# Inputs laid out by the host, small first weight pieces, and clears on GpSimd, in a kernel of two attention blocks

## The chip, the cores and the metric

The kernel runs on one core of one Trainium2 chip. The metric is the device time of one execution in microseconds (us), measured for whole executions; lower is better. A profile is one execution recorded by the hardware profiler; its span (first to last instruction) is about 1.7 us shorter than the measured time of the same execution. Engines: PE (TensorE, matmuls), PEld (its weight loads), DVE (VectorE), ACT (ScalarE), POOL (GpSimd), SP (SyncE, which here only issues transfers). Runs of one kernel scatter by about 1%; a run over 1.5% above the fastest of its kernel is called slow and is left out of every ratio. Work that the host does beforehand is not in this time.

## The reference, cut to what matters

Two attention blocks on 2048 tokens of width 640, with 32 heads of 20, bf16 inputs; their outputs are put side by side.

```
A: q, k, v = x@wq, x@wk, x@wv ; 4 segments of 512 tokens
   within a segment: causal softmax attention
   plus a memory read  phi(q)@M / (phi(q)@z)  gated per head by sigmoid(beta); M, z grow with each segment
   output @ wo
B: q, k, v = x@wqkv ; softmax over a causal window of 256 tokens ; output @ wo
```

The softmax exponentials are the largest single group of the profile (297.9 us): 2 x 32 heads of scores must pass through ACT.

## The kernel before

Work is cut into eight chunks of 512 tokens (A0, B0, A1, B1, ...). All instructions are emitted in an order that a small list scheduler inside the program chooses while the program is built. It keeps an estimated clock for each engine (`f.pe`, `f.act`, `f.dve`, ...), estimated times at which loaded data is there (`mark`), and a chain of pseudo-random choices that starts anew from a given seed every ten score batches:

```python
ORDER = (29069, 0, 182751, 884974, 439894, 0, 228057, 646802, 512461, 772592, 0, 0, 0, 0, 894820)
STRETCH = 10
...
    def stretch(self, i):
        x = i // STRETCH
        self.x = ORDER[x] if x < len(ORDER) else 0

    def pick(self, *of):
        if not self.x:
            return of[0]
        self.x = (self.x * 1103515245 + 12345) % 2147483648
        return of[(self.x >> 12) % len(of)]
```

The engines do not know this clock. Each runs its instructions in the emitted order and waits on semaphores, so an estimate that is wrong does not break the result; it makes an engine wait in front of an instruction while others behind it would have been ready.

The start, which the change rewrites (cut):

```python
        f.dve = f.pool = 6000.0
        f.pe = f.act = 8000.0                    # ns: the scheduler's clock at the first projection
        ...
        nc.vector.memset(zt.bitcast(F32), 0.0)   # 256 columns of qB, for the warm-up
        get_x(0)                                 # dma_start_transpose of x
        # first pieces (172 columns) of wk, wq on ACT's queue, the rest on SP's
        self.load_beta(A_beta)                   # also computes exp(-beta) on ACT
        for x in range(17):                      # warm-up matmuls on zeros
            nc.tensor.matmul(ps[:, :], lhsT=zt[:, 0:P], rhs=zt, start=True, stop=True)
        ...
        nc.vector.memset(self.qB[:, 1:G, :].bitcast(F32), 0.0)
        for t in self.kB:
            nc.vector.memset(t[:].bitcast(F32), 0.0)
        ...
        self.mark(22000.0, 1, "x")               # estimated arrival of B's first x
```

The softmax here doesn't subtract the row's maximum and nothing guards it: scores larger than these inputs give would overflow.

## Time and profile before

| kernel before | |
|---|---|
| median of the first 3 runs | 371.14 us (369.25 to 373.62) |
| span of the profile | 368.6 us |
| ACT busy | 329.8 us, 89% |
| first exponential | 11.53 us |
| ACT's exponentials waiting for PE | 19.8 us (18.1 + 1.5 + 0.2) |

The page of the profile gives busy time, share of the span and number of instructions of each engine:

```profile
PE 335.7 (91%) x6679; PEld 179.0 (49%) x6714; DVE 287.0 (78%) x547; ACT 329.8 (89%) x412; POOL 183.1 (50%) x250
```

Its groups of instructions read: line, engine, operation, output and input with shapes, count, busy us, mean ns, then the idle time just before them and what ended it.

```profile
L654 ACT ACTIVATE pt<-sc 128x1024 bf16<-128x1024 f32 (+1 forms) x328 | 297.9, 1038 | 20.1 <-PE sc L644 18.1
```

ACT's exponentials alone are 297.9 us, and ACT waited only 20.1 us in front of them. PE's 91% says less: it includes warm-up and filler matmuls. The list of waits (who waited for what: total us, times, longest) names what the exponentials waited for:

```profile
ACT pt L654 <- PE sc L644: 18.1, 19, 3.7
...
ACT pt L654 <- PE sc L634: 1.5, 4, 0.5
```

A further 0.2 us makes the 19.8 us of the table. The timeline of the start has start us, duration us, engine, line, operation, tiles, count, and in brackets the idle time before and what ended it:

```profile
7.75 1.26 PE L341 MATMUL m_226<-xT,wk_A 128*32 128x512 bf16 x20
...
9.17 0.64 DVE L349 TENSOR_SCALAR kA<-m_226,rowmask 128x512 bf16<-128x512 f32 x1
...
11.10 0.40 PE L644 MATMUL sc<-qA,kA 32*128 32x512 bf16 x4
...
11.53 7.64 ACT L654 ACTIVATE pt<-sc 128x1024 bf16<-128x1024 f32 x8 [0.81 <-PE sc L644]
...
11.89 0.17 DVE L296 TENSOR_SCALAR t_311<-e_85 128x32 f32<-128x32 f32 x1
```

The first projection starts at 7.75 us, the first exponential at 11.53, and from there ACT is nearly always busy. The waits that stand out in the middle belong to PE, in front of pkT, a transposed copy of phi(k) that is loaded back from a scratch in HBM:

```profile
PE m_1684 L513 <- DMA pkT<-scr_pk_206: 3.0, 1, 3.0
PE m_2862 L513 <- DMA pkT<-scr_pk_207: 2.9, 1, 2.9
```

### The profile page before, as it was taken

Reading aid. Unit: us, or ns where it says so; the run is one execution under the profiler, and the core shown is the slowest. Engines: PE = TensorE matmul, PEld = TensorE weight load, DVE = VectorE, ACT = ScalarE, POOL = GpSimd, SP = SyncE. Lnnn points to the kernel's source line nnn. Section 1 sums busy time; section 2 is a strip of 40 time slices with the busy share of each in tenths; the row PEclk is TensorE's granted clock in tenths of the full one; section 3 lists DMA queues with packets and bytes.
Section 4 is the critical chain, followed back from the end, with each engine's and each line's share of the span. In section 5 each row is a group of like instructions: output and inputs, shape, how many; then the busy total and the mean of one; then the engine's idle time right before and its main releaser. Section 6 shows DMA issues by size and latency. Waiting matters only on the chain.

```text
span 368.6 us, 15618 instructions
## 1 busy us (share of the span) xinstructions
PE 335.7 (91%) x6679; PEld 179.0 (49%) x6714; DVE 287.0 (78%) x547; ACT 329.8 (89%) x412; POOL 183.1 (50%) x250
## 2 busy tenths in 40 slices
PE   8999999969799689889999979998999999998997
PEld 3444354544444434455455544554444555655564
DVE  7667896859798568998799778898797878786760
ACT  1889998959899689999999979999999999997954
POOL 4334442423375335575655555557575655656420
PEclk9999999989999899999999999999999999999999
DMA  9975637789494556249848855366644277529653
GB/s 216 295 260 180 175 111 202 168 196 183 129 221 128 127 145 145 80 138 170 235 122 207 195 135 154 111 139 166 173 117 135 55 191 193 128 75 143 164 125 114
DMA packets 104253, 58.49 MB, mean 159 GB/s; under 512 B 68408, under 2 KB 103608, under 8 KB 104120
## 3 DMA queue, kind: packets, MB, share of 16 engines
q1 hardware_dynamic: 102584, 56.97, 61.8%
q8 instruction: 52, 0.85, 1.0%
q10 hardware_dynamic: 1600, 0.53, 0.6%
q14 instruction: 17, 0.14, 0.1%
HBM read 20.16 MB, written 24.58 MB: 121 GB/s over the span
## 4 chain that ended last, share of the span: by engine, by line
PE 43%; ACT 25%; DMA 12%; DVE 11%; issue 6%; SPq 2%; ACTq 0%; DVEq 0%
ACT pt L654 22%; PE sc L644 6%; DVE tt L739 2%; DMA pkT<-scr_pk_206 2%; DVE st L425 2%; DVE st L201 2%; ACT e L417 2%; PE sc L634 1%; DMA pkT<-scr_pk_207 1%; DMA vbot_177<-vB_166 1%; SPq L377 1%; DMA scr_pk_207<-st 1%; DVE o L758 1%; DMA kB_144<-scr_kB_217 1%; DMA scr_kA_200<-st 1%
## 5 line engine op out<-in xcount | busy, mean ns | idle before, releaser
L654 ACT ACTIVATE pt<-sc 128x1024 bf16<-128x1024 f32 (+1 forms) x328 | 297.9, 1038 | 20.1 <-PE sc L644 18.1
L702 POOL TENSOR_SCALAR_AFFINE_SELECT pt<-pt 128x512 bf16<-128x512 bf16 (+1 forms) x144 | 122.9, 853 | 141.4 <-ACT pt L654 140.6
L698 POOL TENSOR_SCALAR_AFFINE_SELECT pt<-pt 128x512 bf16<-128x512 bf16 x56 | 39.5, 706 | 29.7 <-ACT pt L654 29.7
L758 DVE TENSOR_TENSOR o<-tt,rr 128x320 bf16<-128x320 f32 x64 | 43.2, 674 | 0.8 <-DVE rr L764 0.3
L562 PEld LDWEIGHTS <-xT 128*128 128x128 bf16 x400 | 32.5, 97 | 18.9 <-issue 10.2
L644 PE MATMUL sc<-qA,kA 32*128 32x128 bf16 (+3 forms) x512 | 35.8, 302 | 2.0 <-ACT pt L654 1.2
L820 PEld LDWEIGHTS <-oT 128*128 128x128 bf16 x280 | 24.0, 97 | 15.2 <-issue 5.6
L644 PEld LDWEIGHTS <-kA 32*128 32x128 bf16 x512 | 10.8, 92 | 28.2 <-issue 26.0
L683 DVE TENSOR_TENSOR pt<-pt,hmask 128x2048 bf16<-128x2048 bf16 (+1 forms) x20 | 21.1, 1054 | 0.4 <-ACT pt L654 0.4
L777 POOL TENSOR_TENSOR o<-o,u 128x320 bf16<-128x320 bf16 x24 | 20.1, 836 | 0.0
L644 PE MATMUL sc<-qB,kB_143 32*128 32x64 bf16 (+3 forms) x416 | 18.4, 232 | 0.7 <-ACT pt L654 0.7
L764 DVE RECIPROCAL rr<-tt 128x16 f32<-128x16 f32 x88 | 18.4, 231 | 0.6
L425 DVE SCALAR_TENSOR_TENSOR st<-st,e 128x512 bf16<-128x512 bf16 x25 | 18.3, 738 | 0.0
L716 PEld LDWEIGHTS <-vA 128*32 128x32 bf16 x512 | 11.1, 96 | 13.2 <-issue 1.5
L644 PE MATMUL sc<-qB,kB_144 32*128 32x64 bf16 (+3 forms) x480 | 15.4, 213 | 1.3 <-ACT pt L654 1.1
L417 ACT ACTIVATE e<-st 128x512 bf16<-128x512 bf16 x25 | 15.6, 685 | 0.0
L758 DVE TENSOR_TENSOR u<-tt,rr 128x320 bf16<-128x320 f32 x24 | 15.1, 629 | 0.0
L644 PEld LDWEIGHTS <-kB_143 32*128 32x128 bf16 x416 | 7.9, 92 | 12.9 <-issue 11.6
L399 PEld LDWEIGHTS <-wBq 128*128 128x128 bf16 x100 | 8.6, 97 | 11.0 <-issue 3.5
L399 PEld LDWEIGHTS <-wBk 128*128 128x128 bf16 x100 | 8.5, 97 | 10.1 <-issue 2.6
L716 PEld LDWEIGHTS <-vB_171 128*32 128x32 bf16 x480 | 10.0, 96 | 6.5 <-issue 3.4
L716 PEld LDWEIGHTS <-vB_166 128*32 128x32 bf16 x416 | 9.7, 99 | 7.0 <-issue 1.6
(745 smaller groups left out, 676.8 us busy)
## 6 DMA issues: line engine op xcount, KB each, us to landing
out_dram<-ot SPq DMA_DIRECT2D x31, 160.0 KB
wv_A<-in_A_wv_dram SPq DMA_DIRECT2D x2, 400.0 KB
wBk<-in_B_wqkv_dram SPq DMA_DIRECT2D x1, 800.0 KB
wBq<-in_B_wqkv_dram SPq DMA_DIRECT2D x1, 800.0 KB
wBv<-in_B_wqkv_dram SPq DMA_DIRECT2D x1, 800.0 KB
scr_wo_A<-in_A_wo_dram SPq DMA_DIRECT2D x4, 200.0 KB
wo_A<-scr_wo_A SPq DMA_DIRECT2D x1, 800.0 KB
scr_wo_B<-in_B_wo_dram SPq DMA_DIRECT2D x4, 200.0 KB
```

The costliest lines, as they stand in the source:

```text
L417: nc.scalar.activation(out=e[:], in_=x, func=ACT.Exp)
L425: nc.vector.scalar_tensor_tensor(out=out, in0=x, scalar=0.0, in1=e[:], op0=ALU.max, op1=ALU.add)
L562: nc.tensor.matmul(ps[:, c0:c0 + w], lhsT=xT[:, kt, tt * P:(tt + 1) * P], rhs=w_ap[:, kt, a:a + w], start=(kt == 0), stop=(kt == self.KT - 1))
L644: nc.tensor.matmul(ps[j // 2][:, j % 2, c0:c0 + 64 * nb], lhsT=k[rows, g, P * kc:P * kc + P], rhs=q[rows, g, 64 * b0:64 * (b0 + nb)], star ...
L654: nc.scalar.activation(out=pt[:, 2 * i:2 * i + 2, 0:hi], in_=ps[i][:, :, 0:hi], func=ACT.Exp, scale=self.scale)
L683: nc.vector.tensor_tensor(out=pv, in0=pv, in1=m, op=ALU.min)
L698: nc.gpsimd.affine_select(out=blk, in_=blk, pattern=[[0, r], [-1, w]], compare_op=ALU.is_ge, fill=self.zero, base=-1, channel_multiplier=1)
L702: nc.gpsimd.affine_select(out=blk, in_=blk, pattern=[[0, r], [1, w]], compare_op=ALU.is_ge, fill=self.zero, base=128 - w, channel_multipli ...
L716: nc.tensor.matmul(O[HD * j:HD * j + HD, c:c + 64 * nb], lhsT=self.vcols(v, h // 16 if vk[0] == "v" else 0, vt, h, HD), rhs=rhs[j], start= ...
L758: nc.vector.tensor_tensor(out=out, in0=a, in1=b, op=ALU.mult)
L777: nc.gpsimd.tensor_tensor(out=dst, in0=dst, in1=u[:], op=ALU.add)
L820: nc.tensor.matmul(ps[0:w, 0:320], lhsT=oT[:, m, x:x + w], rhs=wo[:, m, 320 * hf:320 * hf + 320], start=(m == 0), stop=(m == self.KT - 1))
```

## The change

The intent is to start earlier and to relieve SP and the DMA engines. The host transposes x per chunk, packs each weight matrix so that a partition's row is contiguous, pads it, and permutes the rows of wo. So eight transposing loads of x become plain ones, and the eight copies of wo through a scratch in HBM go. The first two head groups of wk and wq come as small separate pieces (`hk`, `hq`), nine warm-up matmuls stand in place of 17, and the clears of B's buffers move from DVE to GpSimd. The scheduler's clock and its estimates of loads are set to the new start; the seeds stay as they are. The diff, cut to its core:

```diff
+NWARM = 9
+WK, WQ, WV = (7300.0, 10900.0), (8600.0, 12000.0), (9800.0, 13200.0)
@@ load_wo2 (weights of the last output projection)
-        for j in range(4):
-            self.nc.sync.dma_start(out=self.wk_A[HD * j:HD * j + HD, :, 0:self.D], in_=self.scr_wo[...])
-        self.f.on_dma(4, 1430.0)
+        self.nc.sync.dma_start(out=self.wk_A[:, :, 0:self.D], in_=self.w["wo2"])
+        self.f.on_dma(1, 2400.0)
@@ load_x
-        self.nc.sync.dma_start_transpose(out=t[:], in_=x2d[c * L:(c + 1) * L, :])
+        for a, b in zip(cuts, cuts[1:]):
+            self.nc.sync.dma_start(out=t[:, a:b, :], in_=x4[c, :, a:b, :])
@@ beta: its exponential moves from load_beta to consts_beta, which is emitted later
@@ the scheduler's clock and estimates
-        f.dve = f.pool = 6000.0
-        f.pe = f.act = 8000.0
+        f.dve = f.pool = 5000.0
+        f.pe = f.act = 5500.0
-                self.mark(f.on_dma(1, 100.0, f.pe, 2900.0, 2100.0) + 50.0, n, "x")
+                self.mark(f.on_dma(1, 1900.0, f.pe, 500.0, 1100.0) + 50.0, n, "x")
-        self.mark(22000.0, 1, "x")
-        f.sp = f.ring = 19000.0
+        self.mark(14000.0, 1, "x")
+        f.sp = f.ring = 15000.0
-                while late and f.pe > 12000.0:
+                while late and f.pe > 8000.0:
@@ clears
-        nc.vector.memset(self.qB[:, 1:G, :].bitcast(F32), 0.0)
-        for t in self.kB:
-            nc.vector.memset(t[:].bitcast(F32), 0.0)
+        for t in (self.kB[0][:], self.qB[:, 1:G, :]):
+            nc.gpsimd.memset(t.bitcast(F32), 0.0)
-        nc.gpsimd.memset(self.MZb[:], 0.0)                    # on GpSimd before too, but earlier
-                nc.vector.memset(t[:].bitcast(F32), 0.0)      # vtop, vbot
+                nc.gpsimd.memset(t[:].bitcast(F32), 0.0)
+        nc.gpsimd.memset(self.kB[1][:].bitcast(F32), 0.0)
+        nc.gpsimd.memset(self.MZb[:], 0.0)
... (load_w, load_parts, layout() on the host, and the passing of the arrays are cut)
```

## The prediction

> **What bounds it now.** ScalarE's exponentials. In the table of busy time ACT has 329.8 of 368.6 us (89%); the pt exponentials alone are 297.9 us (328, mean 1038 ns). PE's 91% contains warm-up and filler matmuls. In the list of waits by engine, ACT loses only 18.1 us waiting for score matmuls, with three waits above 2 us. The remaining ACT idle is mostly the start (the timeline has the first exponential at 11.53 us; ACT worked 2.1 us before it) and the tail after 354 us (output copies waiting for PE). So the change pays where it moves the first exponential, or removes a wait of ACT in the middle.
>
> **The start, before.** 17 warm-up matmuls (0.43 us each, 0.22 from about 6.5 us) run from 1.26 to 7.5 us. Then k0, q0, k1 (1.08 us each) run from 7.75, the first score at 11.10. DMA bytes begin near 2.5 us and flow at 290 GB/s with the engines full until 24 us. Transposed x plus the first wk and wq pieces are 1.07 MB: about 3.7 us, an estimate from that rate, so landed near 6.3.
>
> **After.** Nine warm-ups end at about 5.1 us. k0 needs the first 3/5 of x (393 KB) and hk (220 KB), sharing the engines with hq. At 290 to 340 GB/s (both seen in the trace) I estimate 4.6 to 5.2 us landed for that and about 6.3 for all of x and hq. The Trainium skill ("DMA: Bandwidth & Descriptors", Issuing engines are not separate DMA queues) says the queues of SP and ACT share 16 engines, so the small pieces sent on ACT slow x; the 290 GB/s with both queues at work agree. k0 then starts at 5.3 to 5.7, its first part at the cold rate, and the first exponential comes at about 9.5 us: 2 us earlier. Order of instructions on PE is unchanged here (k0, q0, k1, score, q1).
>
> **Moved and removed elsewhere.**
> - Four 1.8 us-class clears (kB twice 1.76, qB 1.55, two of 0.62) leave DVE, idle a third of that time: worth nothing on the critical path. On GpSimd, at the 0.93 ns per element of its MZb clear, all clears take about 7.7 us (estimate) and end near 12 us, just as the first mask is due.
> - SyncE loses eight x transposes that held its queue 2.8 to 5 us each, about 29 us in all, and the eight copies of wo to scratch. Stores behind them leave sooner, but the large waits of PE in the middle (pkT 3.0 and 2.9 us) come from another transpose, which stays. I allow 0 to 1 us.
> - The order of instructions is re-dealt everywhere: the scheduler's clock starts elsewhere but its per-stretch seeds are kept. On ACT six more evacuation copies (net about +1.8 us at 0.43 to 0.6 us each); on PE 20 fewer fillers. If the seeds were chosen for the old order, part of that choice is lost.
>
> **Sum.** -2 us start, -1 us DMA and queue, +0.5 us evacuations on ACT that no wait absorbs, -0.5 us fewer gaps: 368 us against 371.1. Range 363.5 to 372. Faster by over 2%: 0.12; within 2%: 0.85; slower: 0.03.
>
> **What would show it.** First exponential at 9.2 to 10.2 us in the timeline; the gain there carried to ACT's later work (same exponential 1.5 to 3 us earlier at 60, 150, 300 us); ACT busy about 331 us; no DVE clear; ACT's waits on scores still 15 to 20 us, with the pkT waits present.
>
> **What would make it wrong.** wv landing after 13 us and stalling PE and the scores; masks late behind GpSimd's clears; the re-dealt order opening new ACT gaps (slower), or the freed SyncE queue removing most of the middle waits (then over 2% faster).

## More of the kernel before

The projections of the first chunk write k through DVE and q through ACT, and a score batch is followed by its exponentials:

```python
    def proj_direct(...):                        # 20 matmuls: 5 row tiles x 4 column strips
        ...
        if what == "k":
            nc.vector.tensor_scalar(out=dst[:, g, :], in0=ps[:, :], scalar1=self.rowmask, ...)
        else:
            t = self.evac(dst[:, g, :], ps[:, :], 512, 612.0)      # ACT or DVE, by the scheduler's clock

    def score_batch(...):
        ...
            nc.scalar.activation(out=pt[...], in_=ps[i][...], func=ACT.Exp, scale=self.scale)
```

## The result, and the profile after

The changed kernel takes 383.27 us (median of 4 runs, 381.83 to 390.01) where the kernel before takes 370.29. The ratio is 1.0366, with a 95% interval of 1.0311 to 1.0420: slower by 3.7%. Ratios in this document are those of fast runs of one kernel against fast runs of the kernel before in the same rounds, so they are not quite the ratios of the medians quoted. The means of the fast runs give every other ratio of this document to within 0.001; for the changed kernel they give 1.032 (382.79 over 370.87 us). So its loss is known as 3.2 to 3.7%, and comparisons with 1.0366 are good to half a per cent.

The page of the changed kernel (span 382.0 us), busy times and the group of the exponentials:

```profile
PE 336.0 (88%) x6648; PEld 178.3 (47%) x6686; DVE 281.9 (74%) x537; ACT 332.0 (87%) x415; POOL 191.7 (50%) x255
...
L648 ACT ACTIVATE pt<-sc 128x1024 bf16<-128x1024 f32 (+1 forms) x328 | 298.9, 1048 | 32.4 <-PE sc L638 24.3
```

The exponentials cost the same (298.9 us), ACT has 2.2 us more work in all, and its span has grown by 13.4 us. So 11.2 us of the loss is idle time of ACT, and the list of its waits names it: the exponentials waited 32.0 us (24.3 + 6.9 + 0.8) against 19.8.

```profile
ACT pt L648 <- PE sc L638: 24.3, 19, 3.3
ACT pt L648 <- PE sc L628: 6.9, 6, 3.6
...
ACT pt L648 <- PE m L393: 0.8, 1, 0.8
```

The timeline of the start shows first the gain, then its loss:

```profile
5.33 3.69 PE L335 MATMUL m<-xT,pqA 128*32 128x512 bf16 x60
...
8.73 2.99 DVE L288 TENSOR_SCALAR t<-e 128x32 f32<-128x32 f32 x1 [1.07 <-ACT e L286]
...
8.99 1.81 POOL L1062 MEMSET kB<- 128x2048 f32 x1
...
9.38 3.77 ACT L648 ACTIVATE pt<-sc 128x1024 bf16<-128x1024 f32 x4 [0.68 <-PE sc L638]
...
10.73 0.95 POOL L1063 MEMSET MZb<- 128x1024 bf16 x1
...
13.23 0.74 DVE L343 TENSOR_SCALAR kA<-m,rowmask 128x512 bf16<-128x512 f32 x1
...
14.03 1.26 PE L335 MATMUL m<-xT,wk_A 128*32 128x512 bf16 x20 [3.16 <-DVE kA L343]
...
16.44 5.61 ACT L648 ACTIVATE pt<-sc 128x1024 bf16<-128x1024 f32 x6 [3.29 <-PE sc L638]
```

The first exponential comes at 9.38 us, 2.16 us earlier. But the little DVE operation that took 0.17 us before now takes 2.99 us, and it ends just when GpSimd's last clear ends (10.73 + 0.95 = 11.68). The copy of k stands behind it in DVE's order and is done only at 13.97 us, PE stands 3.16 us in front of its next projection, and ACT stands 3.29 us.

It is useful to follow the same work through both traces. The table gives the start of the n-th exponential, read from each trace:

| n-th exponential | before, us | changed, us | difference |
|---|---|---|---|
| 0 | 11.53 | 9.38 | -2.16 |
| 8 | 19.75 | 20.07 | +0.33 |
| 16 | 28.49 | 30.07 | +1.58 |
| 64 | 87.31 | 89.58 | +2.26 |
| 136 | 167.15 | 170.78 | +3.63 |
| 200 | 233.17 | 238.88 | +5.71 |
| 280 | 310.10 | 316.70 | +6.60 |
| 288 | 316.83 | 328.26 | +11.44 |
| 327 (last) | 352.79 | 365.45 | +12.66 |

So the loss is not one event. Some 3.7 us go in the first 30 us, 5 us in small steps, nearly 5 us at once near 320 us, and 1.2 us after that. The windows there (stretch, its length, busy us of PE, PEld, DVE, ACT and POOL with counts, granted PE clock, DMA share, GB/s) show what a wait of PE does:

```profile
318.00:320.00 2.00, 1.31 (x30) 0.64 (x22) 2.00 (x7) 2.00 (x3) 1.23 (x2) 1.00 0.81 79
320.00:322.00 2.00, 0.00 (x0) 0.00 (x0) 0.62 (x2) 0.47 (x1) 1.68 (x4) 1.00 0.93 263
322.00:324.00 2.00, 1.15 (x37) 0.67 (x37) 0.00 (x0) 0.00 (x0) 0.60 (x1) 0.84 0.04 12
324.00:326.00 2.00, 2.00 (x107) 1.63 (x104) 0.64 (x2) 1.08 (x2) 0.00 (x0) 0.50 0.03 8
```

PE stood until 322.85 us in front of an output projection whose transposed input (oT) had not landed; every score matmul behind it stood too, ACT ran dry, and then PE worked for 3.4 us at half its clock (0.50). In all, PE's clock was halved for 14.3 us of this profile and for 7.1 us of the one before. Those 7.2 us more can have cost at most half of that, 3.6 us (an estimate from the clock records), of the 13.4 us lost.

### The profile page after: what moved, and what is told of

It is laid out like the page before. It is cut to its first block, busy times and chain, and to the rows that moved or that the text cites. A ratio compares the mean times of both kernels' runs of the same rounds, so it can differ in the third digit from the quotient of the medians.

```text
span 382.0 us, 15554 instructions
## 1 busy us (share of the span) xinstructions
PE 336.0 (88%) x6648; PEld 178.3 (47%) x6686; DVE 281.9 (74%) x537; ACT 332.0 (87%) x415; POOL 191.7 (50%) x255
## 4 chain that ended last, share of the span: by engine, by line
PE 37%; DVE 19%; ACT 19%; DMA 12%; issue 7%; SPq 3%; POOL 1%; ACTq 0%; DVEq 0%; POOLq 0%
ACT pt L648 17%; PE m L393 11%; PE m L710 6%; PE sc L638 5%; PE m L814 5%; DVE tt L733 4%; PE m L556 3%; DVE o L752 3%; PE m L335 2%; DVE st L419 2%; DMA oT<-scr_o 2%; DVE vA L568 2%; DMA out_dram<-ot 2%; DMA pkT<-scr_pk 2%; DMA scr_pq<-st 2%
## 5 line engine op out<-in xcount | busy, mean ns | idle before, releaser
L648 ACT ACTIVATE pt<-sc 128x1024 bf16<-128x1024 f32 (+1 forms) x328 | 298.9, 1048 | 32.4 <-PE sc L638 24.3
L733 DVE STREAM_TRANSPOSE tt<-m 128x512 f32<-128x512 f32 x88 | 62.3, 713 | 38.7 <-PE m L710 34.0
L203 DVE CAST st<-m 128x512 bf16<-128x512 f32 x51 | 34.7, 681 | 12.6 <-PE m L393 10.2
L638 PE MATMUL sc<-qB,kB 32*128 32x64 bf16 (+3 forms) x896 | 30.1, 223 | 5.1 <-ACT pt L648 2.4
L814 PE MATMUL m<-wo_A,oT 128*128 128x320 bf16 x160 | 27.2, 302 | 4.2 <-DMA oT<-scr_o 3.5
L556 PE MATMUL m<-wBv,xT 128*128 128x320 bf16 (+2 forms) x200 | 27.0, 273 | 2.6 <-DVE tt L733 1.5
L556 PE MATMUL m<-wv_A,xT 128*128 128x320 bf16 (+2 forms) x200 | 27.4, 276 | 1.0 <-DVE vA L568 0.8
L710 PE MATMUL m<-pt,vB 128*32 128x64 bf16 (+3 forms) x896 | 24.8, 230 | 3.1 <-DVE tt L733 0.7
L393 PE MATMUL m<-xT,wBk 128*128 128x512 bf16 x88 | 24.5, 381 | 2.2 <-DVE tt L733 1.5
L393 PE MATMUL m<-xT,wBq 128*128 128x512 bf16 x88 | 24.0, 380 | 2.4 <-DVE tt L733 0.9
L638 PEld LDWEIGHTS <-kA 32*128 32x128 bf16 x512 | 11.2, 92 | 31.8 <-issue 27.2
L710 PE MATMUL m<-pt,vA 128*32 128x256 bf16 (+3 forms) x512 | 23.3, 302 | 0.7 <-DVE tt L733 0.7
```

The source lines that it names most:

```text
L203: nc.vector.tensor_copy(out=out, in_=in_)
L393: nc.tensor.matmul(ps[:, :], lhsT=w_ap[:, kt, m * P:(m + 1) * P], rhs=xT[:, kt, :], start=(kt == 0), stop=(kt == self.KT - 1))
L556: nc.tensor.matmul(ps[:, c0:c0 + w], lhsT=xT[:, kt, tt * P:(tt + 1) * P], rhs=w_ap[:, kt, a:a + w], start=(kt == 0), stop=(kt == self.KT - 1))
L638: nc.tensor.matmul(ps[j // 2][:, j % 2, c0:c0 + 64 * nb], lhsT=k[rows, g, P * kc:P * kc + P], rhs=q[rows, g, 64 * b0:64 * (b0 + nb)], star ...
L648: nc.scalar.activation(out=pt[:, 2 * i:2 * i + 2, 0:hi], in_=ps[i][:, :, 0:hi], func=ACT.Exp, scale=self.scale)
L710: nc.tensor.matmul(O[HD * j:HD * j + HD, c:c + 64 * nb], lhsT=self.vcols(v, h // 16 if vk[0] == "v" else 0, vt, h, HD), rhs=rhs[j], start= ...
```

## The experiments

Three parts of the change can be at fault: the loads, the clears, and the order of instructions that the scheduler deals when its clock and estimates change. My theory was that the order costs most of it and that GpSimd's clears cost the head start; the rivals were the loads (plain transfers colliding with others) and the clears alone. With the old clock and estimates, the new loads give the old order on every engine: apart from the loads, the warm-ups and the clears, only beta's exponential stands three ACT instructions later. With the new clock and estimates, the old loads likewise give the new order. So order and loads can be crossed.

In the table, us is the median of all runs of a kernel. The ratio is to the kernel before, with its 95% interval.

| label | loads | order | large clears | us | ratio |
|---|---|---|---|---|---|
| (changed kernel) | new | new | GpSimd | 383.27 | 1.0366 (1.0311 to 1.0420) |
| new_loads_old_order | new | old | GpSimd | 368.81 | 0.9892 (0.9795 to 0.9990) |
| old_loads_new_order | old | new | DVE | 381.47 | 1.0257 (1.0173 to 1.0341) |
| after_dve | new | new | DVE | 380.89 | 1.0222 (1.0121 to 1.0323) |
| before_gp | old | old | GpSimd | 368.44 | 0.9911 (0.9826 to 0.9995) |
| best_of_both | new | old | DVE | 367.22 | 0.9959 (0.9923 to 0.9994) |
| before_noseed | old | old estimates, seeds 0 | DVE | 374.50 | 1.0146 (1.0093 to 1.0199) |
| after_noseed | new | new estimates, seeds 0 | GpSimd | 382.56 | 1.0347 (1.0301 to 1.0393) |
| after_seeds4 | new | fresh seeds | GpSimd | 376.17 | 1.0198 (1.0158 to 1.0238) |
| after_wo2est | new | new until late | GpSimd | 380.56 | 1.0307 (1.0236 to 1.0378) |
| after_dve_wo2est | new | new until late | DVE | 377.59 | 1.0217 (1.0143 to 1.0291) |
| after_all_seeds12 | new | fresh seeds | DVE | 368.78 | 0.9981 (0.9912 to 1.0049) |
| before_seeds12 | old | fresh seeds | DVE | 372.44 | 1.0093 (1.0020 to 1.0167) |
| fresh_a | new | fresh seeds | DVE | 379.87 | 1.0283 (1.0217 to 1.0348) |
| fresh_b | new | fresh seeds | DVE | 372.56 | 1.0114 (1.0048 to 1.0179) |
| fresh_c | new | fresh seeds | DVE | 372.30 | 1.0088 (1.0030 to 1.0146) |

The first row is the result above. The others come from four sessions, on chips 11, 11, 9 and 7, in which the kernel before had medians of 370.6, 369.6, 368.5 and 368.4 us; so ratios are compared across sessions, times only within one. The profiles of new_loads_old_order, after_dve and after_dve_wo2est fell in slow runs. The starts of the first two are read below, before their first stretch at half clock (78.9 and 79.7 us); one comparison of later parts says that it rests on slow runs.

### Crossing loads and order

The first run keeps the changed kernel but for the scheduler's inputs:

```diff
-WK, WQ, WV = (7300.0, 10900.0), (8600.0, 12000.0), (9800.0, 13200.0)
+WK, WQ, WV = (0.0, 0.0), (0.0, 0.0), (12000.0, 12000.0)
-        f.pe = f.act = 5500.0
+        f.pe = f.act = 8000.0
... (f.dve, f.sp, the marks of x, on_dma of x and wo2, and late, all as in the kernel before)
```

> The changed kernel's loads, first pieces, nine warm-ups and clears on GpSimd, but the scheduler's clock and estimates as in the kernel before, so PE, ACT, DVE and POOL run the old order of instructions. Theory 1 (the re-dealt order costs the time beyond the start): 369 to 373 us, near the kernel before. Rival (the plain loads or the clears cost it): 380 to 384 us, near the changed kernel. ACT's first exponential near 9.5 us in both; the stretched DVE operation near 9 to 12 us stays in both.

It took 368.81 us, ratio 0.9892: just under the range of theory 1, no slower than the kernel before, and 4.6% under the changed kernel's ratio, with the same loads, the same warm-ups and the same clears. The rival "loads or clears" falls as the main cause. One detail of the expectation missed: the small DVE operation was not stretched to 3 us. In this order it came at 12.12 us, after the last clear, and took 0.60 us.

The second run is the mirror: the kernel before, with the scheduler's inputs of the changed kernel.

> The kernel before with its transposed loads, 17 warm-ups and clears on DVE, but the scheduler's clock and estimates of the changed kernel, so the new order of instructions. Theory 1: 378 to 386 us. Rival (loads or clears): 369 to 373 us.

It took 381.47 us, ratio 1.0257, inside the range of theory 1. The new order alone, on untouched loads, costs 2.6%. Both halves of the crossing agree: the order is the main cause. The waits of ACT in this kernel, where neither loads nor clears were touched:

```profile
ACT pt L655 <- PE sc L645: 22.6, 18, 4.1
ACT pt L655 <- PE sc L635: 4.9, 5, 2.3
```

That is 27.5 us against 19.8 in the kernel before. The delay grows through the whole run: its 8th exponential is 0.8 us earlier than in the kernel before (18.93 us), its 200th 5.2 us later (238.41) and its last 10.4 us later (363.16). The clock explains little of this: PE ran at half clock for 10.2 us here and 7.1 us in the kernel before, worth at most 1.6 us (estimate).

### The clears

The changed kernel with the three large clears back on DVE; PE's, ACT's and SP's orders are unchanged:

```diff
-        for t in (self.kB[0][:], self.qB[:, 1:G, :]):
-            nc.gpsimd.memset(t.bitcast(F32), 0.0)
+        for t in (self.kB[0][:], self.qB[:, 1:G, :], self.kB[1][:]):
+            nc.vector.memset(t.bitcast(F32), 0.0)
...
-        nc.gpsimd.memset(self.kB[1][:].bitcast(F32), 0.0)
```

> The changed kernel with the three large clears (kB twice, qB) back on DVE, where it idles until 6.9 us. Theory (GpSimd's clears hold up DVE's first small operation from 8.73 to 11.72 us): the stretched operation falls to about 0.2 us, ACT's wait of 3.3 us at 13 to 16 us is gone, span 2 to 4 us shorter, 379 to 381 us. Rival (that wait is caught up later because ACT is not the limit there): within 1 us of the changed kernel.

The median of 380.89 us lies in the range expected, and the ratio fell from 1.0366 to 1.0222; but the two intervals overlap, so the size of the gain is uncertain. The timeline of this kernel, DVE and ACT:

```profile
8.32 0.18 DVE L288 TENSOR_SCALAR t<-e 128x32 f32<-128x32 f32 x1
...
9.91 0.74 DVE L343 TENSOR_SCALAR kA<-m,rowmask 128x512 bf16<-128x512 f32 x1
...
10.03 3.77 ACT L648 ACTIVATE pt<-sc 128x1024 bf16<-128x1024 f32 x4 [1.74 <-PE sc L638]
14.55 5.60 ACT L648 ACTIVATE pt<-sc 128x1024 bf16<-128x1024 f32 x6 [0.75 <-PE sc L638]
```

The stretched operation is back at 0.18 us and the second group of exponentials starts at 14.55 us instead of 16.44, although the first starts 0.65 us later because the DVE clears now delay the first copy of k. The Trainium skill ("SBUF — State Buffer", Who interferes with whom) states that GpSimd and a DVE instruction in a two-port mode share one port pair, which is held for a whole instruction while the other fully blocks, and that copies and tensor_scalar can run in such a mode. The trace agrees: an operation on 32 columns took 2.99 us beside GpSimd's clears and 0.18 without. It adds one thing: the DVE operation began during one clear and waited through two more that followed it without a gap. In three more profiles with these loads and clears (after_noseed, after_wo2est, after_seeds4) it began at 8.73, 8.94 and 9.35 us and ended each time at 11.73, with the last clear.

The same move in the kernel before, nothing else changed:

> The kernel before with its clears on GpSimd as the change puts them, nothing else. If DVE is held while GpSimd clears, the first k copy at 9.2 us or the beta operations near 11.9 us stretch and ACT gets a new wait of 1 to 3 us before 20 us: 371 to 374 us. If the clears are done before DVE needs its port: 370 to 371 us, as before.

Ratio 0.9911: no loss. The timelines say why. GpSimd's last clear was over before DVE's small operation began:

```profile
10.72 0.94 POOL L1070 MEMSET MZb<- 128x1024 bf16 x1
...
12.20 0.17 DVE L296 TENSOR_SCALAR t<-e 128x32 f32<-128x32 f32 x1
```

So the same clears are harmless here and harmful in the changed kernel, where the operation comes 3.5 us earlier (8.73 us; it came at 9.70 us with the new order alone and at 12.12 us with the new loads alone). That this run came out 0.9% under the kernel before is within what runs differ by: its interval reaches 0.9995, and three of its four runs had a mean granted clock of 0.995 or 1.000 where the kernel before mostly had 0.986 to 0.991.

### Seeds

The seeds were kept by the change. Were they chosen for the old order? With all of them zero:

```diff
-ORDER = (29069, 0, 182751, 884974, 439894, 0, 228057, 646802, 512461, 772592, 0, 0, 0, 0, 894820)
+ORDER = (0,)
```

> The kernel before, loads untouched, with all scheduler seeds set to zero: another order of the same work. If the order of before was selected and any other order costs some per cent: 376 to 386 us. If the order matters little and only the changed kernel's order is bad: 369 to 373 us.

> The changed kernel with all seeds set to zero. If the changed kernel's 383 us is simply what an unselected order costs: 378 to 388 us, like the kernel before without seeds. If the kept seeds harm the new order in particular: 370 to 376 us.

Without seeds the kernel before loses 1.5% (374.50 us) and the changed kernel nothing (1.0347 against 1.0366). So the seeds were worth something in the old order and nothing in the new. But neither expectation came out as a whole: 374.50 us lies between its two ranges, and after_noseed, though at 382.56 us in its first range, is not "like the kernel before without seeds", which stays 2% under it. The lost choice of seeds is a part of the order's cost, not all of it.

Then seeds chosen anew for the changed kernel, by a search on the scheduler's own estimate of the end (a number of the program, not a measurement):

> The changed kernel with seeds chosen anew by search on the scheduler's own estimate, which for this order is 9 us shorter than for the changed kernel. If a fresh choice recovers the order's loss: 368 to 375 us. If the scheduler's estimate does not tell good orders from bad ones on the chip: 378 to 388 us.

376.17 us, ratio 1.0198: better by 1.7%, but outside the range expected, between the two theories. It was faster although its profile has six half-clock stretches of PE with 23.9 us in all, where the changed kernel has 14.3 and the kernel before 7.1 (read from the clock records of the three traces).

### One estimate

The largest step in the table of exponentials, near 320 us, was a wait for a transposed load in a stretch where the scheduler had just counted the last weight load as one transfer of 2400 ns instead of four of 1430. That is one line to put back; it leaves the order alone until PE's matmul 5387 of 6688:

```diff
-        self.f.on_dma(1, 2400.0)
+        self.f.on_dma(4, 1430.0)
```

> The changed kernel with one number of the scheduler put back: the estimate for the last weight load (four transfers of 1430 ns instead of one of 2400). The load itself stays one transfer. The order is the same until PE's matmul 5387 of 6688. Theory (the shorter estimate makes the scheduler place output projections before their transposed input has landed): PE's wait of 3.5 us for oT near 320 us and ACT's wait of 3.6 us near 324 us are gone, the half-clock stretch there too, 376 to 380 us. Rival (the single large transfer itself holds up the other loads, whatever the estimate): both waits stay, 381 to 384 us.

380.56 us, ratio 1.0307, above the range expected. The wait for oT shrank from 3.5 to 1.7 us, but ACT still ran dry nearby (2.52 us at 326.56). The 288th exponential came 11.56 us late against the kernel before, where the changed kernel had 11.44; but this execution had lost 2.7 us more at its start (below), so the step itself is the better measure. From the 280th to the 288th exponential the kernel before took 6.73 us, the changed kernel 11.56 and this one 9.10: about half of the step went. With the clears on DVE the same line changed nothing: 11.14 us without it (after_dve), 11.10 with it (after_dve_wo2est), both in slow runs. My theory of that one number is not borne out.

This run shows something else. It has the changed kernel's start, instruction for instruction, and the same hold of DVE. The windows of the two (columns as above), the changed kernel first:

```profile
12.00:14.00 2.00, 0.00 (x0) 0.00 (x0) 1.91 (x10) 1.15 (x2) 1.18 (x2) 1.00 1.18 342
14.00:16.00 2.00, 1.97 (x25) 0.88 (x24) 1.23 (x2) 0.00 (x0) 0.31 (x1) 1.00 1.07 407
16.00:18.00 2.00, 2.00 (x27) 1.24 (x27) 0.77 (x2) 1.56 (x2) 0.00 (x0) 1.00 1.06 435
18.00:20.00 2.00, 1.95 (x27) 0.90 (x29) 1.14 (x2) 2.00 (x3) 1.09 (x1) 1.00 1.00 410
```

And after_wo2est:

```profile
12.00:14.00 2.00, 0.00 (x0) 0.00 (x0) 1.91 (x10) 1.36 (x2) 0.99 (x2) 0.79 1.16 340
14.00:16.00 2.00, 1.95 (x20) 0.69 (x19) 0.59 (x1) 0.00 (x0) 0.52 (x1) 0.50 1.07 410
16.00:18.00 2.00, 2.00 (x17) 0.72 (x13) 0.75 (x1) 0.00 (x0) 0.00 (x0) 0.50 1.02 419
18.00:20.00 2.00, 2.00 (x20) 1.59 (x13) 0.68 (x1) 1.60 (x2) 0.00 (x0) 0.50 1.05 432
```

PE stood 3.16 us in one run and 2.97 in the other. In the first its clock stayed at 1.00; in the second it was halved from 13.2 us for 6.8 us, and the 8th exponential came at 22.79 us instead of 20.07. The Trainium skill ("TensorE: Matmul & The Clock Gate", What's actually happening) describes this: the clock is halved after an idle window of about 3.4 us, the window runs freely, and a busy window brings the clock back. The runs agree only in part. The halved stretches last 3.4 or 6.8 us, one or two such windows, and similar waits sometimes halve the clock and sometimes not. But the waits of PE that came with a halving were shorter than such a window: 2.97 us here, 2.46 us in after_seeds4 (halved from 13.98 us) and 1.97 us in fresh_b (from 14.01 us). So a wait of 3 us cost 3 us in one execution and about 5.7 in another. This may be much of the 1% by which runs of one kernel differ: of before_gp, the run with a mean granted clock of 1.000 took 365.39 us and the profiled one, with 10.2 us at half clock, 370.39, and half of 10.2 us is close to the difference. That is one pair, not a test.

The two repairs together:

> The two repairs together: large clears on DVE and the old estimate of the last weight load; everything else as changed. If they add: 2 us and 4 us under the changed kernel, 375 to 378 us. If one hides the other: 379 to 381 us.

377.59 us, ratio 1.0217, the same as the clears on DVE alone (1.0222). The time lies in the range for "they add", but by luck: no worth of the estimate can be seen here. The pair in one session gives a second size for the clears: fast runs of 380.5 us on average with them on GpSimd (four runs), 376.6 with them on DVE (three), 3.9 us, with hardly any overlap but few runs.

### Fresh seeds again, and for the kernel before

> The two repairs, and seeds chosen anew on the scheduler's own estimate, which is 9 us under that of the changed kernel. If a fresh choice is worth what it was worth alone (about 7 us): 367 to 372 us. If the choice on the estimate and the repairs take away the same waits: 373 to 377 us.

368.78 us, ratio 0.9981. In one session, with the same loads and clears, nothing but the seeds took the ratio from 1.0217 to 0.9981. With the clears moved back, the order alone can give back the rest of the loss. But is that what a fresh choice gives, or luck?

> The kernel before with seeds chosen anew by the same search, estimate 6 us under that of the kernel before. If the estimate tells good orders from bad: 363 to 367 us. If the seeds that the kernel before has were better than their estimate says (chosen by times on the chip): 370 to 378 us.

The kernel before, given seeds by the same search, becomes slower (372.44 us, 1.0093; its second range was 370 to 378), although the scheduler's estimate promised 6 us less. Three more sets for the changed kernel, each from another search, with estimates within 1 us of each other:

> The changed kernel, large clears on DVE, all of the changed estimates kept, seeds from a second search (estimate 342 us, as for the fresh seeds already run). If a fresh choice on the estimate recovers the order's loss in general: 366 to 371 us. If the one fresh set that reached the time of the kernel before was luck: 373 to 380 us.

> As fresh_a with seeds of a third search from other starting points (estimate 343 us). General recovery: 366 to 371 us; luck: 373 to 380 us.

> As fresh_a with the old estimate of the last weight load and seeds of a fourth search (estimate 342 us). General recovery: 366 to 371 us; luck: 373 to 380 us. A run under 365 us would be a version better than every one so far.

Ratios 1.0283, 1.0114 and 1.0088. Of the four fresh orders with clears on DVE, one reaches the kernel before, three are 0.9 to 2.8% slower. The full recovery was a lucky order, though two of the three fell a little short of the 373 us I had written for luck: most fresh orders gave back a part. The estimate does not tell such orders apart on the chip. Orders of the same work spread over 3%, which is more than the change could gain.

### The parts that helped, put together

The new loads, first pieces and nine warm-ups, in the old order, with the three large clears on DVE and beta's exponential issued early as before:

```diff
+        self.e32 = self.cp.tile([P, H], F32, name="e32")       # right after load_parts()
+        nc.scalar.activation(out=self.e32[:], in_=self.beta[:], func=ACT.Exp, scale=-1.0)
... (the scheduler's inputs as in new_loads_old_order, the clears as in after_dve)
```

> The new loads, first pieces and nine warm-ups, with the old order of instructions, the three large clears back on DVE and beta's exponential issued early as before. If the three parts add up (head start of the loads kept, no held DVE, old order): first exponential near 10 us, ACT's wait of 2.15 us near 15 us gone, 366 to 369 us with the same number of half-clock stretches as before, so 1 to 4 us under the kernel before. If the head start is absorbed later by a wait that ends at the same time whatever the start: 370 to 371 us.

In five rounds its median is 367.22 us where the kernel before has 369.63, ratio 0.9959 (0.9923 to 0.9994): 0.4% faster on average. The time is in the range expected, but the interval only just leaves out no gain, as that of before_gp did (0.9995), which I put down to scatter; and new_loads_old_order, with 0.9892, is not slower. So it is clearly faster than the changed kernel and at least as fast as the kernel before; more is not shown. ACT's timeline at the start, first of new_loads_old_order (clears on GpSimd):

```profile
10.04 1.94 ACT L648 ACTIVATE pt<-sc 128x1024 bf16<-128x1024 f32 x2 [0.81 <-PE sc L638]
...
16.07 3.77 ACT L648 ACTIVATE pt<-sc 128x1024 bf16<-128x1024 f32 x4 [2.15 <-PE sc L638]
```

then of best_of_both:

```profile
10.04 3.77 ACT L647 ACTIVATE pt<-sc 128x1024 bf16<-128x1024 f32 x4 [1.73 <-PE sc L637]
14.77 3.77 ACT L647 ACTIVATE pt<-sc 128x1024 bf16<-128x1024 f32 x4 [0.96 <-PE sc L637]
19.11 5.85 ACT L647 ACTIVATE pt<-sc 128x1024 bf16<-128x1024 f32 x6 [0.57 <-PE sc L637]
```

The wait of 2.15 us is down to 0.96, not gone as expected. The two kernels differ in the clears and in beta's exponential; which of these did it was not separated. Of the head start of 1.50 us (10.04 against 11.53), 0.63 is left at the 8th exponential and still at the 48th (66.58 us against 67.22). Later it cannot be followed: the 64th is 0.6 us late, the 136th 3.7 us early.

## Why the prediction was wrong, point by point

- **The bound and the start were right.** ACT's exponentials bound the kernel, and the first one came at 9.38 us (predicted about 9.5, range 9.2 to 10.2). k0, the first head group's projection of k, started at 5.33 us (predicted 5.3 to 5.7). That the queues of SP and ACT share the same 16 DMA engines (the Trainium skill, "DMA: Bandwidth & Descriptors", Issuing engines are not separate DMA queues, which the prediction cites) does not contradict the trace; no run here tests it.
- **"-2 us start" was kept only as far as the first exponential.** In the changed kernel it was gone by the 8th. In best_of_both, where no clear holds DVE, 0.63 us of 1.50 was still there at the 48th, and the whole kernel gained 0.4%, about 1.5 us. The sum's "-1 us DMA and queue" was not tested by itself; the two terms together were to bring 3 us.
- **The clears were mis-judged.** The prediction called them "worth nothing on the critical path" and costed them only as late masks. It did not ask what GpSimd's clears do to DVE while they run. They held one small DVE operation for 2.99 us, and with it PE and ACT. Measured: 1.0 to 1.4% between the changed kernel (1.032 or 1.0366) and after_dve, with overlapping intervals, and 3.9 us by the pair in one session; at the 8th exponential the profiles show 1.9 us (20.07 against 18.18). The hold itself is in the traces; its worth over the whole kernel is rough. In the old order, where DVE's small operation came after the clears, they cost nothing that could be measured.
- **The step that failed is the sum's two terms for the re-dealt order: "+0.5 us evacuations on ACT that no wait absorbs, -0.5 us fewer gaps".** They were to cancel. Measured, the new order costs 2.6% (old_loads_new_order against the kernel before: fast runs of 381.0 and 371.4 us on average, so nearly 10 us where the sum has 0), and again 2.6% between best_of_both and after_dve, which differ in beta's exponential too. In the profiles it is the wait of ACT's exponentials for PE, 27.5 us in old_loads_new_order and 32.0 in the changed kernel against 19.8 (predicted 15 to 20), not the extra evacuations (ACT busy 332.0 us, predicted 331). The prediction even named the re-dealing ("the re-dealt order opening new ACT gaps"), but as a risk, and gave it 0.03.
- **The same exponential was to be 1.5 to 3 us earlier at 60, 150 and 300 us.** It was later: by 2.5 us at the 48th (69.74 against 67.22 us), 2.2 at the 120th, 6.6 at the 272nd.
- **The sizes, step by step.** In ratios: loads and head start 0.9959 (best_of_both); the order takes it to 1.0222 (after_dve); the clears to 1.0366 (the changed kernel). Such a chain ends at the changed kernel by construction, so only independent measurements support it: 1.0257 on the old loads for the middle step, and 3.9 us (1%) for the last. The first step also holds the early exponential of beta, which after_dve has not.
- **What stays open.** Why this order is bad is shown only as a sum of waits: in the profiles ACT's exponentials wait 17.9 to 22.2 us for PE in best_of_both, after_all_seeds12, fresh_b and fresh_c (ratios 0.9959 to 1.0114) and 27.5 to 32.0 us in fresh_a, old_loads_new_order and the changed kernel (1.0257 to 1.0366). What in the order makes PE late is not shown. The one wait that I singled out, near 320 us, shrank in one pair of profiles and stayed in the other when its estimate was put back. The seeds explain a part (1.5% in the kernel before). No rule was found that tells a good order from a bad one before it runs; the scheduler's own estimate does not, since four orders with nearly equal estimates measured 0.998 to 1.028.

## What to carry to other kernels

In a kernel whose instruction order comes from a scheduler fed with estimates, changing any estimate deals a new order of all later work, and here orders of the same work differed by 3%: test a change with the order held first, and do not judge it by one order that was chosen on an estimate. Choosing the order by times on the chip is the obvious next step; no run here tried it. Moving work to an idle engine is not free by itself: look at what the busy engines do at that time. Clears on GpSimd cost nothing measurable in one order and about 3.9 us in another. A stall of PE near 3 us can cost nearly twice its length when the clock is halved with it (3.0 us became about 5.7 here).

## What the Trainium skill lacked or had wrong

- "SBUF — State Buffer" says that who starts first holds the shared ports for one whole instruction. It does not say that a DVE instruction can be passed over by several GpSimd instructions in a row: here it began at 8.73 us, during one clear, and ended at 11.72 us, after two further clears (8.99 to 10.80 and 10.73 to 11.68; the profile's times on GpSimd are rough).
- "TensorE: Matmul & The Clock Gate" (What's actually happening) has the clock halved after at least one idle window of about 3.4 us. Here shorter waits of PE came with a halving (2.97, 2.46 and 1.97 us), while one of 3.16 us did not; two executions with nearly the same wait (3.16 and 2.97 us) were 2.7 us apart at the 8th exponential.
- No page deals with list schedulers inside a kernel. Here seeds that were worth 1.5% under one set of estimates were worth nothing under another, and orders of the same work differed by up to 3%.
